# Attention, a mixture of attention experts and a channel mixing in one kernel: other tables for the order of the experts' stage

## The chip, the core and the metric

The kernel runs on one core of a Trainium2 chip. A core has TensorE (PE, matrix products), VectorE (DVE), ScalarE (ACT) and GpSimd (POOL), each with a queue of its own that runs in order, and SyncE (SP), from whose queue the DMAs of this kernel are issued. Results of TensorE land in PSUM and are copied from there to SBUF by VectorE or ScalarE. The metric is the device time of one execution in microseconds (us). It was 1124.65 us for the kernel before, the median of three runs (1122.15 to 1127.39).

## The reference

Three layers follow each other, all on 4 batches and in float32 (the weights of the third layer come as 64-bit floats and are decoded on the chip):

```python
# 1: attention, 8 heads of 64, 1152 rows pooled by 2 to 576 queries
q_pool = q.reshape(B, H, S // 2, 2, D).mean(axis=3)
attn_out = softmax(scale * q_pool @ k.T) @ v                 # (4, 8, 576, 64)
x = attn_out.transpose(0, 2, 1, 3).reshape(4, 576, 512)
# 2: four experts, each a causal attention head of width 64; a row takes two
logits = x @ w_gate                                          # top 2 of 4, softmax of those
for e in range(4):
    q, k, v = x @ wq[e], x @ wk[e], x @ wv[e]
    ye = softmax(causal(scale * q @ k.T)) @ v @ wo[e]
    out += gate_e * ye
# 3: mixing along the rows by rank 32, then along the channels
u = out + (out.T @ U @ V).T
result = u + relu(u @ w_ch1) @ w_ch2                         # 512 -> 2048 -> 512
```

## The kernel before

**The stages.** A first stage computes layer 1 in 16 units (batch times pair of heads) and ends near 480 us. The experts' stage follows, near 480 to 735 us. The channel mixing is the rest; its first units run at the end of the experts' stage. Float32 precision is kept by splitting an operand into a rounded part and a remainder (xh and xl, oh and ol, x2h and x2l, uh and ul, hh and hl) and by adding three products: a copy on ScalarE gives the first part (L226) and a subtraction on VectorE the second (L227).

**A job and its units.** The experts' stage has 8 jobs: 4 batches times 2 expert pairs (ep). Job j has 8 units, one for each half of the queries and each block of 128 keys. A unit's `score` is products st (L871, L872 and the causal mask L876), exp on ScalarE, and sums of the exponentials over the blocks on GpSimd (acc, L885 and L888); its `pv` multiplies with the values (L896). After the last unit of a half, `post_a` sums acc over the partitions (L903), `post_r` and `post_b` turn that into a reciprocal times gate (L432 to L445) and scale the result (L913) into oh and ol.

**What is prepared beside it.** While job j runs, `prep_b(j + 1)` makes the next job's inputs as steps of their own: `cuts` split x by column block (4 steps), `vals` project the values and the gate of a new batch (6 steps), and `projs` (15 steps) are four projections (keys then queries, columns 0 to 320 and 320 to 576), nine score maxima `mxs(t)`, and two `dmax` that write the shifted maxima into q2a and q2b (L399). A maximum is one product (L817) of 64 queries of two heads with up to 512 key columns, and a reduction on VectorE (L820, L824). The maxima get wider with t: 64 to 576 columns; those over 512 are two pieces. The second scores product, L872, reads q2a and q2b, so a job's scores wait for its dmax.

**The mixing.** `mix(b)` has 11 steps: x2(0) to x2(4), tt, hh(0) to hh(4). x2(t) multiplies oh and ol of a batch by wo (6 products of 512 columns), copies the result, splits it into x2h and x2l and adds it to a running product with MUP (L948). tt takes the sum to SBUF as ts (three ACT copies L954, one VectorE subtraction L955). hh(t) multiplies ts back (L961), adds it to x2 (L962), and after the last two the rows are written to u_d in DRAM, from where the channel mixing loads them.

**The tail.** Beside the last job the first weights of the channel mixing are loaded and decoded from 64 bits (`split`, raw to w: six VectorE operations L243 to L248 per half block of 128x512, then a copy on ACT and a subtraction on GpSimd L227), the first rows are turned (L1155) and split, and `mlp(0, fi)` computes the first layer (`up`, L1199, relu L1202, remainder hl L1203) and, one unit later, the second (`down`, L1218).

**What sets the order.** `stream` walks through ticks, three for two units, and issues the units' scores and products and the steps placed at that tick. A step's tick is from a table: CUT_AT, VAL_AT and PRJ_AT[1] for a job that brings a new batch, PRJ_AT[0] for the second pair of a batch, counted from the start of the job beside which the preparation runs; MIX_AT for the mixing of the batch before; MIX_END for the mixing of the last batch, counted from the last job's start like EARLY (opening of the pools and loads of the tail), CW (four weight blocks), CT (turn) and CM (four `mlp` units). The lists are read in the order of the steps given above. A job is 12 ticks long.

```python
for at, g in zip((CUT_AT, VAL_AT, PRJ_AT[1]) if new else ([], [], PRJ_AT[0]), steps):
    place(side, [(3 + t * .75 if j == 0 else t, y) for t, y in zip(at, g)], s0)
if j % EP == 0 and j:
    place(side, list(zip(MIX_AT, mix(j // EP - 1))), s0)
...
place(side, list(zip(MIX_END, mix(B - 1))), sl)
```

This stage isn't under the manual schedule of the others: the framework's scheduler takes the issued order and arranges each engine's row again by its estimates and by when buffers come free. What each engine then has in its row is shown with the change.

**Buffers.** All projections, values, maxima, denominators, output products, hh, turns and first layers write into three PSUM buffers named ms, in turn: a product waits until the third one back has been read. pv has two PSUM buffers, of which the mixing holds one for its running product. x2h and x2l have two buffers each, and so has the raw 64-bit weight.

Of the kernel before, what the change touches and what calls it, by code (L numbers as in the profile page):

```python
# [38 lines left out]
XP_AT = [18, 19, 21, 22, 25, 26, 27, 28, 29, 30, 31, 32, 33, 34, 35]  # L39


CUT_AT = [0, 0, 0, 0]
VAL_AT = [0, 2, 5, 5, 6, 13]
PRJ_AT = [[3, 7, 0, 4, 4, 8, 4, 9, 5, 9, 7, 7, 7, 9, 10], [6, 6, 0, 4, 6, 6, 6, 6, 8, 8, 6, 6, 14, 13, 14]]

MIX_AT = [9, 11, 11, 11, 11, 17, 18, 24, 20, 28, 32]
MIX_END = [14, 17, 18, 21, 23, 25, 39, 32, 31, 41, 38]

EARLY = 5
CW = [7, 20, 23, 37]  # L50
CT = 7
CM = [7, 25, 32, 49]

LATE = 0

# [4 lines left out]
def place(side, steps, t0):  # L60
    for t, g in steps:
        side.setdefault(t0 + int(t), []).append(g)
# [24 lines left out]
def stream(units, side):  # L87

    n = len(units) // 2
    later = {}

    def run(t):
        for g in later.pop(t, []) + side.get(t, []):
            x = g()
            for d, y in enumerate(x if isinstance(x, tuple) else (x,)):
                if callable(y):
                    later.setdefault(t + 1 + d, []).append(y)

    i = 0
    end = max(side, default=0)
    while i <= n or later or 3 * i <= end:
        if i < n:
            units[2 * i][0](0)
            units[2 * i][0](1)
        run(3 * i)
        if i < n:
            units[2 * i + 1][0](0)
        run(3 * i + 1)  # L110
        if i < n:
            units[2 * i + 1][0](1)
        if i % 2 == 0 and 0 < i <= n:
            for x in units[2 * i - 4:2 * i]:
                x[1]()
                if x[2]:
                    for d, y in enumerate(x[2]):
                        later.setdefault(3 * i + 4 + d, []).append(y)
        run(3 * i + 2)
        i += 1  # L120
# [3 lines left out]
def kernel(  # L124
# [795 lines left out]
    def x2_tile(b):  # L920
        if b not in X2:
            X2[b] = xpool.tile([P, NTT - 1, DM], F32, name="x2", tag="x")
        return X2[b]
# [55 lines left out]
    for j in range(NJ):  # L979
        s0 = SA + j * ns  # L980
        units += [unit_b(j, h, kt) for h in range(2) for kt in KT[h]]
        if j + 1 < NJ:
            new = (j + 1) % EP == 0
            steps = prep_b(j + 1, "sv" if new else "s")
# [4 lines that stand above are left out]
    sl = SA + (NJ - 1) * ns  # L989
    place(side, list(zip(MIX_END, mix(B - 1))), sl)  # L990

# [11 lines left out]
    def u_tiles(x, pool_, **kw):  # L1003
        if x == 1:
            u = pool_.tile([P, NC * T], F32, name=f"u{x}", **kw)
            U[x] = u[:, :NS * DM].rearrange("p (s d) -> p s d", s=NS)
            SPARE.append(u[:, NS * DM:NS * DM + 2 * TB].rearrange("p (y t) -> p y t", y=2))
        else:
            U[x] = pool_.tile([P, NS, DM], F32, name=f"u{x}", **kw)
        UH[x] = pool_.tile([P, NC, TB], F32R, name=f"uh{x}", **kw)  # L1010
        UL[x] = pool_.tile([P, NC, TB], F32R, name=f"ul{x}", **kw)
# [65 lines left out]
    def split(fi):  # L1077
        for x, g in enumerate([weights(fi, x) for x in range(2)]):
            gs, end = g()
            for y in gs:  # L1080
                y()
            end()
            keep(fi, x)
# [61 lines left out]
    def load_u(x):  # L1145
        if x > 1:
            U[x] = ct["u"].tile([P, NS, DM], F32, name="u")
        nc.sync.dma_start(U[x], u_d[x * TB:(x + 1) * TB, :].rearrange("(s p) d -> p s d", p=P))
# [9 lines left out]
    def turn(x, c):  # L1158
        turned.add((x, c))
        cut(turn_(x, c), UH[x][:, c, :], UL[x][:, c, :])  # L1160
# [72 lines left out]
    def mlp(x, fi):  # L1233
        hl = up(x, fi)
        if pend:
            down(*pend.pop())
        pend.append((x, fi, hl, [W[fi][:, 1, a, :] for a in range(2)]))
        if x == 0 and fi < 4:
            for y in range(fi + 1):
                if 1 in U and (1, y) not in turned:  # L1240
                    turn(1, y)
# [14 lines left out]
    def seven(p, k, late, more):  # L1256
# [37 lines left out]
        if late:  # L1294
# [21 lines left out]

    place(side, [(EARLY, open_early), (EARLY + 1, lambda: load_u(0)),
                 (EARLY + 4, lambda: (x2_tile(B - 1), u_tiles(1, xpool, tag="x"), load_u(1)) and None)], sl)
    place(side, [(t, lambda fi=fi: split(fi)) for fi, t in enumerate(CW)], sl)
    place(side, [(CT, lambda c=c: turn(0, c)) for c in range(NC)], sl)  # L1320
    place(side, [(t, lambda fi=fi: mlp(0, fi)) for fi, t in enumerate(CM)], sl)
    stream(units, side)
    n = len(CM)
    NK = NF // 2
# [103 lines left out]
```

## Time and profile before

| | |
|---|---|
| median of three runs | 1124.65 us (1122.15 to 1127.39) |
| the profiled execution | 1122.36 us |
| its span | 1120.6 us |
| mean granted clock of TensorE | 0.992 |
| TensorE busy in the span | 1081.5 us |
| VectorE, ACT, POOL busy | 812.8, 542.3, 614.2 us |
| TensorE busy in 480 to 740 us | 246.85 of 260 us |

The profile is of one execution, read after it by several views: the page with the busy time of each engine and the chain of work that ended last; the busy time by stretches; the waits, by the line that waits and the line it waits for; groups of like instructions by line; and the timeline of single instructions. A figure behind "x" is a count of instructions. A matmul's end is modelled, so that two neighbours overlap in the timeline; the distance of two starts tells how long one takes of TensorE.

### The profile page before, as it was taken

The page shows a single profiled execution, that of the slowest core. Times are in us where ns is not written, and L with a number is a line of the kernel's source. Part 1 is how long each engine was busy: PE and PEld are TensorE (multiplying, and loading weights), DVE is VectorE, ACT ScalarE, POOL GpSimd, SP SyncE. Part 2 cuts the span into 40 slices and gives each one's busy share as a digit, 9 for nine tenths or more (in the row PEclk, how much of TensorE's full clock was granted, in tenths as well). Part 3 has the DMA queues.
Part 4 walks back from the last instruction along what each step waited for, and adds up shares of the span by engine and source line. Part 5 has one row for each costly group of instructions (what it writes and reads, how often), then busy time and mean ns, then how long its engine had stood idle before and what let it go on. Part 6 is the DMA issues. An engine that isn't in the chain of part 4 may idle for free.

```text
span 1120.6 us, 19602 instructions
## 1 busy us (share of the span) xinstructions
PE 1081.5 (97%) x6652; PEld 887.4 (79%) x6652; DVE 812.8 (73%) x1707; ACT 542.3 (48%) x1361; POOL 614.2 (55%) x620
## 2 busy tenths in 40 slices
PE   6999999999999999899999999899998999999998
PEld 4777777777777777678787876689887988998987
DVE  6777777888888777656858588979879455565444
ACT  4555666555555555543454535434445445433231
POOL 6888999988888888854424243200009596800000
PEclk8999999999999999999999999999999999999999
DMA  6878897778777765111203044576754755575431
GB/s 144 193 179 185 184 205 175 171 169 193 171 171 166 172 151 117 43 35 38 58 23 106 14 117 148 165 225 195 233 197 169 245 179 188 183 264 202 169 123 57
DMA packets 135157, 171.50 MB, mean 153 GB/s; under 512 B 72464, under 2 KB 88848, under 8 KB 133008
## 3 DMA queue, kind: packets, MB, share of 16 engines
q1 hardware_dynamic: 135056, 170.24, 55.7%
q8 instruction: 53, 0.87, 0.3%
q14 instruction: 48, 0.39, 0.1%
HBM read 83.06 MB, written 32.51 MB: 103 GB/s over the span
## 4 chain that ended last, share of the span: by engine, by line
PE 82%; DVE 8%; POOL 4%; issue 2%; ACT 2%; DMA 2%; SPq 0%; POOLq 0%; ACTq 0%; DVEq 0%
PE o L1218 14%; PE pv L626 12%; PE ms L1268 9%; PE ms L745 9%; PE st L606 8%; PE ms L558 7%; PE st L607 6%; PE ms L1199 5%; PE pv L896 2%; PE ms L633 2%; DVE mp L560 1%; PE ms L506 1%; PE ms L817 1%; DVE xl L227 1%; PE st L872 1%
## 5 line engine op out<-in xcount | busy, mean ns | idle before, releaser
L618 POOL TENSOR_TENSOR acc<-acc,pt 128x576 f32<-128x576 f32 x224 | 319.6, 1427 | 34.3 <-ACT pt L608 18.9
L608 ACT ACTIVATE pt<-st 128x288 f32<-128x288 f32 x576 | 220.0, 409 | 186.1 <-PE st L607 139.3
L560 DVE TENSOR_REDUCE mp<-ms 128x1 f32<-128x384 f32 x432 | 215.1, 549 | 57.6 <-PE ms L558 55.6
L626 PE MATMUL pv<-pt,vr 128*64 128x288 f32 x1152 | 152.3, 409 | 0.0
L558 PE MATMUL ms<-kn,bd 128*128 128x384 f32 x432 | 145.3, 358 | 3.6 <-DVE mp L560 1.7
L626 PEld LDWEIGHTS pv<-pt,vr 128*64 128x64 f32 x1152 | 80.1, 137 | 55.4 <-issue 3.8
L1218 PE MATMUL o<-w,hh 128*128 128x512 f32 x384 | 120.2, 394 | 2.0 <-ACT hh L1202 1.7
L606 PE MATMUL st<-q1a,s1a 128*128 128x288 f32 x288 | 93.7, 325 | 2.8 <-ACT pt L608 2.0
L606 PE MATMUL st<-q1b,s1b 128*128 128x288 f32 x288 | 92.6, 321 | 0.2 <-ACT pt L608 0.2
L558 PEld LDWEIGHTS ms<-kn,bd 128*128 128x128 f32 x432 | 79.9, 191 | 14.8 <-DVE mp L560 6.3
L607 PE MATMUL st<-q2a,s2a 128*128 128x288 f32 x288 | 85.5, 297 | 0.0
L607 PE MATMUL st<-q2b,s2b 128*128 128x288 f32 x288 | 85.1, 296 | 0.0
L1268 PE MATMUL ms<-bc,w 128*128 128x384 f32 x432 | 84.7, 341 | 0.0
L1218 PEld LDWEIGHTS o<-w,hh 128*128 128x128 f32 x384 | 71.5, 188 | 13.9 <-ACT hh L1202 2.0
L1268 PEld LDWEIGHTS ms<-bc,w 128*128 128x128 f32 x432 | 77.6, 190 | 3.0
L1218 PE MATMUL o<-w,hl 128*128 128x512 f32 x192 | 75.5, 393 | 0.9 <-DVE hl L1203 0.9
L606 PEld LDWEIGHTS st<-q1a,s1a 128*128 128x128 f32 x288 | 54.4, 189 | 25.2 <-issue 21.7
L888 POOL TENSOR_TENSOR acc<-acc,pt 128x576 f32<-128x576 f32 (+4 forms) x48 | 45.9, 956 | 49.7 <-ACT pt L879 47.8
L1199 PE MATMUL ms<-uh,w 128*128 128x384 f32 x256 | 71.8, 340 | 1.3 <-ACT sg L1173 1.0
L1218 PE MATMUL o<-w,hs 128*128 128x512 f32 x288 | 71.4, 392 | 0.0
L615 POOL TENSOR_TENSOR acc<-pt 128x576 f32<-128x576 f32 x32 | 50.7, 1586 | 34.8 <-ACT pt L608 34.8
L227 POOL TENSOR_TENSOR bc<-sg,bc 128x384 fp32r<-128x384 f32 x6 | 7.0, 1171 | 106.8 <-ACT bc L226 104.2
(241 smaller groups left out, 2416.9 us busy)
## 6 DMA issues: line engine op xcount, KB each, us to landing
raw<-in_moe_w_ch_dram SPq DMA_DIRECT2D x32, 512.0 KB
w_d<-cb SPq DMA_DIRECT2D x40, 256.0 KB
qr<-in_q_dram SPq DMA_DIRECT2D x16, 576.0 KB
vr<-in_v_dram SPq DMA_DIRECT2D x16, 576.0 KB
s1a<-kn SPq DMA_DIRECT2D x31, 288.0 KB
s1b<-kn SPq DMA_DIRECT2D x31, 288.0 KB
kr<-in_k_dram SPq DMA_DIRECT2D x30, 288.0 KB
wv<-v_d SPq DMA_DIRECT2D x8, 1024.0 KB
```

Of the source, the lines that this page charges most:

```text
L558: nc.tensor.matmul(ps[:, :384], BD[i % 2][:, t, :], KN[i % 2][:, c * 384:c * 384 + 384], start=True, stop=True)
L560: nc.vector.tensor_reduce(st["mp"][:, t, c:c + 1], ps[:, :384], axis=X, op=ALU.max)
L606: nc.tensor.matmul(ps[:, :HT], pr.S1[a][:, ks], pr.Q1[a][:, qs], start=True, stop=False)
L607: nc.tensor.matmul(ps[:, :HT], pr.S2[a][:, ks], pr.Q2[a][:, qs], start=False, stop=True)
L608: nc.scalar.activation(c["pt"][:, a, :], ps[:, :HT], AF.Exp, scale=0.0625)
L615: nc.gpsimd.tensor_add(t, acc[i, h], c["pt"])
L618: nc.gpsimd.tensor_add(acc[i, h], acc[i, h], c["pt"])
L626: nc.tensor.matmul(o[64 * a:64 * a + 64, :HT], vr[:, a, kt, :], c["pt"][:, a, :], start=(kt == 0), stop=(kt == NKT - 1))
L745: nc.tensor.matmul(ps, stat[x][s], mov[x][m], start=(x == 0 and y == 0), stop=(x == n - 1 and y == 2))
L1199: nc.tensor.matmul(ps[:, :TB], W[fi][:, 0, a, cs], m[:, c, :], start=(c == 0 and y == 0), stop=(c == NC - 1 and y == 2))
L1218: nc.tensor.matmul(ob[x][s_], hl[m][:, r], w2[a], start=(n == 0 and y == 0), stop=(n == NF - 1 and y == 2))
L1268: nc.tensor.matmul(ps[:, :TB], w[:, i * HD2 + c * P:i * HD2 + c * P + P], b[:, j, c, :], start=(c == 0 and y == 0), stop=(c == HC - 1 and ...
```

## The change

Only tables are changed. The same instructions are issued, in other places. Step by step: the projections of the second pair of a batch (PRJ_AT[0]) start a tick sooner and its maxima are spread up to tick 15; those of a new batch begin with the two key and query projections of columns 0 to 320 at tick 3, and values come from tick 4; the mixing of a batch (MIX_AT) has its x2 one or more ticks sooner and its tt and hh all by tick 19; the last batch's mixing (MIX_END) is spread to tick 94; the tail's tables (EARLY, CW, CT, CM) have other ticks.

```diff
-CUT_AT = [0, 0, 0, 0]
-VAL_AT = [0, 2, 5, 5, 6, 13]
-PRJ_AT = [[3, 7, 0, 4, 4, 8, 4, 9, 5, 9, 7, 7, 7, 9, 10], [6, 6, 0, 4, 6, 6, 6, 6, 8, 8, 6, 6, 14, 13, 14]]
-
-MIX_AT = [9, 11, 11, 11, 11, 17, 18, 24, 20, 28, 32]
-MIX_END = [14, 17, 18, 21, 23, 25, 39, 32, 31, 41, 38]
-
-EARLY = 5
-CW = [7, 20, 23, 37]
-CT = 7
-CM = [7, 25, 32, 49]
+CUT_AT = [0, 0, 0, 1]
+VAL_AT = [4, 4, 4, 5, 6, 12]
+PRJ_AT = [[2, 7, 0, 2, 2, 5, 5, 7, 6, 11, 8, 13, 9, 12, 15], [3, 8, 3, 7, 5, 7, 6, 7, 5, 9, 10, 11, 14, 10, 15]]
+
+MIX_AT = [8, 8, 8, 10, 11, 11, 18, 17, 15, 18, 19]
+MIX_END = [18, 29, 30, 30, 31, 38, 42, 74, 52, 94, 45]
+
+EARLY = 4
+CW = [5, 9, 21, 27]
+CT = 6
+CM = [9, 17, 36, 50]
```

**First place: TensorE beside job 4, the maxima of job 5.** Before, the maxima pieces of 384, 448 and 512 columns (L817) stand among the PV products (L896):

```order
L896 MATMUL pv<-pt,vl_6828 64x288 x2
L896 MATMUL pv<-pt,vl_6828 64x160
L817 MATMUL ms<-knb,bdb 128x384
L817 MATMUL ms<-knb,bdb 128x448
L896 MATMUL pv<-pt,vl_6828 64x160
L896 MATMUL pv<-pt,vl_6828 64x32 x2
L896 MATMUL pv<-pt,vl_6828 64x288
L817 MATMUL ms<-knb,bdb 128x512
L896 MATMUL pv<-pt,vl_6828 64x288
L871 MATMUL st<-q1a_6469,s1a_6461 128x192
```

Now 384 stands behind the PV products and before the output products of the mixing (wo), of which 18 follow in a row:

```order
L896 MATMUL pv<-pt,vl_6828 64x288 x2
L896 MATMUL pv<-pt,vl_6828 64x160 x2
L896 MATMUL pv<-pt,vl_6828 64x32 x2
L896 MATMUL pv<-pt,vl_6828 64x288 x2
L817 MATMUL ms<-knb,bdb 128x384
L745 MATMUL ms<-wo_108,oh_6846 128x512
L745 MATMUL ms<-wo_109,oh_6846 128x512
L745 MATMUL ms<-wo_108,ol_6848 128x512
L745 MATMUL ms<-wo_108,oh_6847 128x512
```

The pieces of 512 and 448 columns moved behind these output products.

**Second place: VectorE ahead of job 4's first scores.** q2a and q2b with 64x320 are written for those scores (L399). Before they stand behind the maxima of 448 and 320 columns and are the last thing before the old job's denominator (L432):

```order
L820 ISA ms,mx<-ms,mask_m 128x448
L820 ISA mx 128x1
L962 TENSOR_TENSOR x_7766<-ms,x_7766 128x512
L820 ISA ms,mx<-ms,mask_m 128x320
L820 ISA mx 128x1
L399 TENSOR_TENSOR q2a_6471<-negid,mx 64x320
L399 TENSOR_TENSOR q2b_6472<-negid,mx 64x320
L432 STREAM_TRANSPOSE d_8185<-ms 128x288
```

Now they stand ahead of steps of the gate (g_) and of the remainder of the second key projection (klob):

```order
L820 ISA ms,mx<-ms,mask_m 128x256
L820 ISA mx 128x1
L387 TENSOR_TENSOR q1a_6469<-ms,q1a_6469 64x256
L387 TENSOR_TENSOR q1b_6470<-ms,q1b_6470 64x256
L399 TENSOR_TENSOR q2a_6471<-negid,mx 64x320
L399 TENSOR_TENSOR q2b_6472<-negid,mx 64x320
L774 TENSOR_REDUCE g_m<-g_d 128x5
L775 TENSOR_SCALAR g_m<-g_m 128x5
L776 RECIPROCAL g_m<-g_m 128x5
L777 TENSOR_TENSOR g_g<-g_d,g_m 128x20
L368 TENSOR_TENSOR klob<-ms,knb 128x256
L432 STREAM_TRANSPOSE d_8199<-ms 128x288
```

The two L399 moved ahead, and the wider maxima behind them.

**Third place: VectorE where the first weight is decoded (dca, dcb from raw).** Before, the decode begins between the remainders of batch 2's mixing (x2l), ahead of its ts (L955) and its additions (L962):

```order
L227 TENSOR_TENSOR x2l<-ms,x2h 128x512 x2
L243 TENSOR_SCALAR dca<-raw 128x512
L246 TENSOR_SCALAR dcb<-raw 128x512
L244 TENSOR_SCALAR dca<-dca 128x512
L227 TENSOR_TENSOR x2l<-ms,x2h 128x512
L245 TENSOR_SCALAR dca<-dca 128x512
L246 TENSOR_SCALAR dcb<-raw 128x512
L247 SCALAR_TENSOR_TENSOR dcb<-dca,dcb 128x512
L248 SCALAR_TENSOR_TENSOR dcb<-raw,dcb 128x512
L243 TENSOR_SCALAR dca<-raw 128x512
L955 TENSOR_TENSOR ts<-pv,ts 32x512
```

Now it comes behind ts and behind four of the five additions:

```order
L955 TENSOR_TENSOR ts<-pv,ts 32x512
L399 TENSOR_TENSOR q2b_6843<-negid,mx 64x256
L962 TENSOR_TENSOR x_9179<-ms,x_9179 128x512
L432 STREAM_TRANSPOSE d_9384<-ms 128x288
L962 TENSOR_TENSOR x_9179<-ms,x_9179 128x512
L434 TENSOR_SCALAR d_9386<-d_9384 128x9
L962 TENSOR_TENSOR x_9179<-ms,x_9179 128x512
L435 RECIPROCAL d_9386<-d_9386 128x9
L962 TENSOR_TENSOR x_9179<-ms,x_9179 128x512
L437 TENSOR_TENSOR d_9386<-d_9386,g_w 128x9
L243 TENSOR_SCALAR dca<-raw 128x512
L246 TENSOR_SCALAR dcb<-raw 128x512
```

The additions moved ahead of the decode. On TensorE, in rows that are not shown, the first layer of the channel mixing's first unit stands at row 3014 of 3926 instead of 3001 of 3932, that of the second at 3032 instead of 3073, and the output products of the last batch, which stood ahead of the second unit's first layer, follow behind it.

## Rows read from the trace of the kernel before

**Rows 1.** The page: busy time by engine; the chain by engine.
```profile
PE 1081.5 (97%) x6652; PEld 887.4 (79%) x6652; DVE 812.8 (73%) x1707; ACT 542.3 (48%) x1361; POOL 614.2 (55%) x620
PE 82%; DVE 8%; POOL 4%; issue 2%; ACT 2%; DMA 2%; SPq 0%; POOLq 0%; ACTq 0%; DVEq 0%
```

**Rows 2.** Busy time by 20 us: stretch, length, engines (instructions), clock, DMA share, GB/s.
```profile
500.00:520.00 20.00, 17.98 (x122) 14.65 (x123) 14.67 (x35) 8.00 (x20) 7.88 (x11) 0.91 0.17 40
...
540.00:560.00 20.00, 18.53 (x120) 13.94 (x119) 18.01 (x47) 9.14 (x23) 7.14 (x9) 1.00 0.25 59
...
600.00:620.00 20.00, 18.58 (x111) 13.54 (x110) 17.65 (x47) 10.00 (x24) 5.83 (x7) 1.00 0.38 111
...
680.00:700.00 20.00, 17.89 (x123) 12.54 (x123) 19.29 (x38) 11.07 (x26) 10.36 (x10) 1.00 0.26 79
700.00:720.00 20.00, 17.28 (x82) 12.42 (x78) 18.86 (x41) 11.51 (x23) 4.35 (x4) 1.00 0.60 192
720.00:740.00 20.00, 19.44 (x95) 16.27 (x96) 16.93 (x31) 5.84 (x12) 3.46 (x3) 1.00 0.50 158
sum 260.00, PE 246.85 PEld 198.15 DVE 194.89 ACT 120.06 POOL 95.35; mean PE 18.99 PEld 15.24 DVE 14.99 ACT 9.24 POOL 7.33
```

**Rows 3.** Waits of TensorE, 480 to 735 us: total us, times, longest.
```profile
PE ms L817 <- DVE mx L820: 4.2, 4, 1.6
PE ms L1155 <- DVE x L962: 1.7, 1, 1.7
PE o L1218 <- ACT hh L1202: 1.7, 1, 1.7
PE st L872 <- DVE q2b L399: 1.6, 3, 0.5
```

**Rows 4.** Busy time by 4 us, columns as in Rows 2.
```profile
504.00:508.00 4.00, 3.44 (x18) 2.60 (x19) 3.60 (x13) 0.77 (x2) 1.45 (x2) 0.70 0.25 59
```

**Rows 5.** Timeline at the maxima of jobs 1 and 5: start, us, instruction, [idle before].
```profile
504.56 0.51 PE L817 MATMUL ms<-knb,bdb 128*128 128x512 f32 x1 [1.62 <-DVE mx L820]
...
608.12 1.67 DVE L227 TENSOR_TENSOR ol<-o,oh 128x288 fp32r<-128x288 f32 x1
608.43 0.82 PE L896 MATMUL pv<-pt,vl 128*64 128x160 f32 x8
610.37 0.50 PE L817 MATMUL ms<-knb,bdb 128*128 128x512 f32 x1 [1.12 <-DVE mx L820]
```

**Rows 6.** Timeline of the tail, single instructions of VectorE and TensorE.
```profile
680.04 0.42 DVE L243 TENSOR_SCALAR dca<-raw 128x512 int32<-128x512 int32 x1
...
711.72 0.63 PE L745 MATMUL ms<-wo,oh 128*128 128x512 f32 x2
...
731.81 0.55 DVE L1203 SCALAR_TENSOR_TENSOR hl<-ms,hh 128x384 fp32r<-128x384 f32 x1
```

**Rows 7.** Groups on VectorE, 480 to 735 us: count, busy us, mean ns, idle before.
```profile
L962 DVE TENSOR_TENSOR x<-ms,x 128x512 f32<-128x512 f32 x16 | 10.8, 680 | 5.4 <-PE ms L961 5.4
L227 DVE TENSOR_TENSOR ol<-o,oh 128x288 fp32r<-128x288 f32 x16 | 10.2, 639 | 3.2 <-ACT oh L226 3.1
L399 DVE TENSOR_TENSOR q2b<-negid,mx 64x320 fp32r<-64x320 f32 x7 | 5.6, 804 | 0.2
L820 DVE CUSTOM_DVE_ANT_0 ms<-ms,mask_m 128x512 f32<-128x512 f32 x7 | 5.0, 717 | 0.0
L955 DVE TENSOR_TENSOR ts<-pv,ts 32x512 fp32r<-32x512 f32 x4 | 2.7, 680 | 5.7 <-PE ms L745 2.8 <-ACT ts L954 2.8
```

**Rows 8.** Timeline ahead of job 4's second scores product.
```profile
589.75 3.30 POOL L888 TENSOR_TENSOR acc<-acc,pt 128x576 f32<-128x576 f32 x3
591.56 1.18 DVE L399 TENSOR_TENSOR q2b<-negid,mx 64x320 fp32r<-64x320 f32 x1
592.79 0.40 PE L872 MATMUL st<-q2b,s2b 128*128 128x288 f32 x1 [0.52 <-DVE q2b L399]
```

**Rows 9.** The line that copies ts: count, ns min/median/max, first and last start.
```profile
L954 ACT ACTIVATE ts<-pv x12: 585/587/589, 568.2 to 718.3; 32x512 fp32r<-32x512 f32 x12
```

## The prediction

> **What bounds the kernel now.** I read the page first, for which engine carries the span. TensorE is busy 97% of it, and 82% of the chain that ended last is TensorE work; VectorE carries 8% of that chain [rows 1]. A new order of the same steps can therefore only win back time in which TensorE pauses or runs slowly. The second view, busy time by 20 us over the stage that the tables govern (480 to 740 us), says how much that is: TensorE is busy 246.85 of 260 us, so 13.15 us are idle, and they sit in few stretches: 2.0 us in 500 to 520, 1.5 in 540 to 560, 1.4 in 600 to 620, and 2.1 and 2.7 in the two stretches of the tail, 680 to 720; VectorE is busiest in just those stretches (18.0 and 17.7 of 20 us in the middle, 19.3 and 18.9 in the tail) [rows 2]. The tail, 680 to 740, has 5.4 us of the idle time and the part ahead of it 7.8. The third view, the waits of TensorE, names them: 4.2 us before a score-maximum product (L817) until VectorE had read an older one (L820), 1.6 us before a score product (L872) until VectorE had written the shifted maxima (q2b, L399), and 1.7 us before a turn (L1155) and 1.7 before a second-layer product (L1218) in the tail [rows 3]. The fourth view is the granted clock: 0.70 in 504 to 508 us, a stretch that begins with the longest of the L817 waits, 1.62 us, in front of the product at 504.56; at 0.70 in 4 us about 1.2 us of work is lost, and TensorE counts as busy there, so this comes on top of the idle time [rows 4, 5]. The ceiling is then near 14.5 us, of which 9 lie ahead of the tail.
>
> **Part 1: the score maxima of the second expert pair of each batch (PRJ_AT).** All projection, value, maxima, denominator and mixing products take turns in three PSUM buffers named ms. Before, the pieces of 384, 448 and 512 columns come within ten instructions of each other, so the third buffer round meets VectorE's queue. At 607 us: VectorE spends 1.67 us in one subtraction (ol) before it reaches the maxima; the eight PV products of 0.82 us are all that covers it; TensorE stands 1.12 us before the 512 piece [rows 5]. The same form stands in jobs 1, 3 and 5 and makes almost all of the 4.2 us. In the new order, the 384 piece is followed by 18 output products of the mixing, and the 512 piece comes behind those. Two output products of 512 columns take 0.63 us where one takes 0.40, so one follows the other by 0.23, and 18 of them cover 4.1 us [rows 6], against 1.67 plus about 0.72 for the longest maximum [rows 5, 7]. The wait goes in jobs 3 and 5. Job 1 has no mixing beside it, so there the pieces have only values and scores between them: I leave 0.5 us. Where a wait goes, the next buffer user is late instead; with the pieces apart I leave 0.2 us in each of the other jobs. Gain 4.2 - 0.5 - 0.4 = 3.3, bounds 1.5 and 4.2.
>
> **Part 2: the shift by the maxima just before the next job's first scores.** Before, the last small maximum (320 columns) and the two L399 of 64x320 stand directly ahead of the first scores that read them: TensorE stands 0.52 us at 592.79 because q2b took 1.18 us instead of the 0.80 that is its mean [rows 7, 8]. Three such waits make 1.6 us [rows 3]. In the new order both L399 stand in VectorE's row behind the 256-column maximum, and TensorE has eight PV products (0.82 us, rows 5), a projection of 12 products and the last scores of the old job ahead of the first reader. That covers two L399 of 1.2 us at their worst but for a little. Gain 1.5, bounds 0.8 and 1.6.
>
> The Trainium skill (SBUF — State Buffer, on the shared port pair) says that a VectorE instruction with two SBUF inputs and a GpSimd instruction that reads SBUF lock each other out for the whole instruction. The trace agrees at this place: q2b (1.18 us) began while GpSimd's accumulation of 3.30 us ran [rows 8]. By that rule a new order decides nothing by itself: each of these operations can again begin under an accumulation, and parts 1 and 2 would come back elsewhere at some 1 us a hit; this is a mechanism of the first rival below.
>
> **Part 3: the clock.** If the 1.6 us pause before the dip is gone, the dip may go too. The trace has just this one in the stage, so I take 0.8 of its 1.2 us; bounds 0 and 1.2 [rows 4].
>
> **Part 4: the smaller pauses ahead of the tail.** Of the 7.8 us idle ahead of the tail, 5.8 are the two waits above; the other 2.0 are shorter pauses, one or two at a line. The same crowding makes them, and products whose modelled ends run into each other may hide some more; I take 1.5, bounds -0.5 and 2.5.
>
> **Part 5: what the new order adds (MIX_AT).** The last maxima now stand between L948 products, and the first hh (L961) follows soon after the last L948. Ahead of it lie three ACT copies of 0.587 us and one subtraction of 0.68, 2.4 us in a chain, counted without the hops between engines [rows 7, 9]; ahead of it on TensorE stand eight PV products and some short scores, between 1.5 and 2.5 us. Queued behind a waiting L961 is the next job's first projection, and so everything. I price it at 0.5 us for each of three batches: a loss of 1.5, bounds 0 and 4. VAL_AT and CUT_AT move the value products and one cut; their copies out of PSUM are the same in number and lie beside projections: nothing, bounds -0.5 and 0.5.
>
> **Part 6: the tail (MIX_END, EARLY, CW, CT, CM).** VectorE is the limit there: in the 51.8 us from the first decode step (680.04) to the fourth unit's hl (731.81) it is busy nearly all the time [rows 2, 6]. The steps are the same in number. New is that four additions of the mixing of batch 2 (L962, 0.68 us each, 2.7 us) stand ahead of the first decode instead of behind it, and that three of the last batch's five hh come after the fourth unit's first layer. The decode starts later by about that, and less of VectorE's work is left behind it. On TensorE the first unit's first layer stands at row 3014 instead of 3001 and the second's at 3032 instead of 3073, so the second unit is asked for before its weights can be decoded: a new wait of 2 to 4 us there, and the output products of the last batch, now behind it, fill what were waits at L1155 and L1218 (3.4 us together) [rows 3]. On SP the DMAs are the same; the one write of batch 2's mixing that the reload of its rows depends on moves with hh, and stays some microseconds ahead of the turn. I take a gain of 1.5, bounds -4 and 5.
>
> **Sum.** 3.3 + 1.5 + 0.8 + 1.5 - 1.5 + 1.5 = 7.1 us, some half of the ceiling. The profiled execution took 1122.36 us (1.8 more than its span) and would take 1115.3; it lies 2.3 us under the median of the runs shown, and from that median, 1124.65, the forecast is 1117.5.
>
> **The rivals.**
> *The waits only move.* VectorE's work is unchanged, and a hit on ol or q2b costs about 1 us wherever an accumulation happens to run; ol shows it in its mean, 0.64 us over 16, against single ones far above [rows 5, 7]. Then parts 1 and 2 give 2.5 instead of 4.8, the clock and part 4 nothing, part 5 costs 2.5, the tail gives 1: a gain of 1, 1123.6. For it: the collisions belong to timing, not to order. Against it: the new order gives up to 4 us of cover where there was 0.8.
> *The tail gives its waits too.* If the turn of the second unit's input and the output products fill the tail as meant, its gain is its whole idle time of 5.4 us instead of 1.5, part 4 gives 2 and part 5 costs nothing: 7.1 + 3.9 + 0.5 + 1.5 = 13, 1111.6. For it: the new order puts TensorE work that needs no decode behind the second unit. Against it: VectorE is as full as before, and full at 95%.
> *Slower: the decode starts late.* One mechanism: the first decode waits in VectorE's row behind the four L962, these wait for hh, hh for ts, and ts for the L948 products between the scores. Up to its start VectorE stands idle with the raw weights landed. Some of a later start is absorbed: 3.4 us of VectorE's work (four L962 and the L955 before them, 0.68 each) are done ahead, 2.0 us (three L962) are left behind, and about 2.5 us are its idle time in 51.8 at 38.2 busy of 40 [rows 2, 6, 7]. From a start that is 8 us later than now, counted from the last-but-one job's first scores, the rest falls on the end. With a start 13 us later and 5 us of collisions between the decode and the accumulations and weight cuts on GpSimd it costs 10 us, against 5 gained ahead: 1129.7. For it: the order does put these ahead. Against: they were the last thing between the jobs before, too, and their wait is a few microseconds.
> *Not what it says.* That the channel mixing begins sooner holds for its second unit, not for its first by the order on TensorE; if the decode decides, nothing begins sooner. This is in the first and the third rival and has no case of its own.
>
> **How the numbers follow.** Forecast 0.44, waits only move 0.27, tail too 0.17, slower 0.12. About 0.5%, 5.6 us, is what a measurement of this kernel can tell from no change. The forecast's own range is 1114 to 1121, of which some 0.32 is more than 5.6 us under the median; with the tail's 0.17 and 0.05 of the first rival that is 0.54 for faster. Same gets the other 0.12 of the forecast, 0.20 of the first rival and 0.02 of the slower one, 0.34; slower 0.12, with 0.02 of the first rival. The range that leaves out 2 in 10 goes from 1109.5 (half of the tail's case below it) to 1126.5.
>
> **What the profile would show.** Part 1 is right if TensorE's waits at L817 on L820 fall from 4.2 to about 1 us, and wrong if they are above 2.5. Part 2: no wait at L872 on q2b. Part 3: no slice at a clock under 0.9 near the second job. Part 5: a wait at L961 on ts in each batch, about 0.5 us. Part 6: VectorE busy over 90% from first decode to the fourth hl, that stretch 45 to 49 us instead of 51.8, and a wait at the second unit's L1199 on its weights. The prediction is wrong if TensorE idles in the stage as long as before, 13 us, or under 5.

## The result: 1.0% faster, and the profile after

The changed kernel took 1110.70 us, the median of six runs (1109.62 to 1115.79); the kernel before, timed beside it, 1124.63 us (1121.47 to 1127.39). The ratio is 0.9898 with a 95% interval of 0.9883 to 0.9913, so the change is worth 11.5 us (9.8 to 13.2). The forecast was 7.1 us and a time of 1117.5; the time lies under the forecast's own range (1114 to 1121) and inside the wider one (1109.5 to 1126.5). The execution whose profile follows took 1115.27 us (span 1113.5), one of the two slower ones of the six. Its first stage, with the same instructions as before, ended 3.2 us later than in the profile of before: the first job's first product of 160 columns starts at 485.59 instead of 482.43. Differences are therefore counted from that product.

Busy time by 20 us after the change, with the columns of [rows 2]:

```profile
500.00:520.00 20.00, 18.76 (x136) 14.79 (x136) 15.85 (x41) 9.27 (x23) 10.48 (x18) 1.00 0.27 64
...
540.00:560.00 20.00, 19.95 (x129) 16.11 (x129) 16.89 (x45) 11.95 (x28) 7.03 (x10) 1.00 0.23 54
...
600.00:620.00 20.00, 19.95 (x126) 15.39 (x125) 17.31 (x39) 13.77 (x30) 5.91 (x7) 1.00 0.13 30
...
680.00:700.00 20.00, 16.50 (x80) 11.45 (x81) 19.32 (x41) 6.39 (x14) 7.51 (x6) 0.91 0.48 151
700.00:720.00 20.00, 18.19 (x81) 14.03 (x81) 18.63 (x37) 10.38 (x20) 4.20 (x3) 1.00 0.44 136
720.00:740.00 20.00, 18.77 (x85) 16.41 (x84) 12.13 (x23) 5.87 (x12) 1.28 (x1) 0.91 0.60 198
```

Ahead of the tail TensorE has almost stopped pausing (18.53 and 18.58 of 20 us became 19.95 twice), and the clock of 0.91 beside the second job is gone. In the tail it pauses as before, and two stretches have a clock of 0.91 that had 1.00 in [rows 2]. Over 480 to 740 us TensorE idles 8.5 us instead of 13.15.

The waits of TensorE after the change, 475 to 730 us (total us, times, longest):

```profile
PE ms L961 <- DVE ul L227: 1.4, 2, 0.9
PE ms L817 <- DVE mx L820: 1.2, 2, 1.0
PE ms L1199 <- POOL w L227: 1.1, 2, 0.6
PE pv L896 <- DVE o L913: 0.9, 1, 0.9
```

The wait at L817 fell from 4.2 to 1.2 us, that at L872 on q2b (1.6) is gone [rows 3]; the new lines are all in the tail. The 1.2 us that are left all stand beside the first job (at 506.94 and 510.20 us).

Now one stretch that holds the same work in both: from the first job's first product of 160 score columns to the last job's. Busy time by stretches, the kernel before and then the changed one:

```profile
482.43:681.08 198.65, 191.39 (x1317) 156.73 (x1316) 138.63 (x393) 92.39 (x225) 74.88 (x153) 0.99 0.25 68
```

```profile
485.59:669.24 183.65, 182.27 (x1318) 155.13 (x1317) 135.84 (x385) 93.81 (x227) 73.92 (x153) 1.00 0.27 73
```

The stretch is 15.0 us shorter with the same number of TensorE instructions but one. TensorE's idle time fell from 7.3 to 1.4 us; the other 9.1 us came out of its *busy* time. From the last job's product to the end of the span the change costs 4.7 us (1120.6 - 681.08 = 439.5 before, 1113.5 - 669.24 = 444.3 after). So the pair of profiles reads: -3.2 in the first stage, +15.0, -4.7, in sum the 7.1 us between the spans.

How can a busy TensorE win 9 us? The group of the PV products (L896) in the same two stretches, count, busy us and mean ns, before and after:

```profile
L896 PE MATMUL pv<-pt,vl 128*64 128x288 f32 (+4 forms) x208 | 24.6, 347 | 0.0
```

```profile
L896 PE MATMUL pv<-pt,vl 128*64 128x288 f32 (+4 forms) x208 | 20.8, 343 | 0.0
```

The mean of one is nearly the same and the busy time of 208 is 3.8 us less. Busy time counts an overlap once, and a matmul's modelled time reaches over the start of the next one, so a group gets shorter when its products stand in fewer rows. They do: by the starts in the traces, another line follows one of the 208 products 20 times before and 13 times after, while inside a row the next product starts 92 and 85 ns later in the mean. This is order, not pause.

Short pauses that the modelled ends reach over are there too. One such place in the kernel before, ahead of the first scores of job 2 (timeline: start, us, instruction):

```profile
532.85 1.31 DVE L399 TENSOR_TENSOR q2a<-negid,mx 64x320 fp32r<-64x320 f32 x1
533.77 0.38 PE L871 MATMUL st<-q1a,s1a 128*128 128x288 f32 x1
534.21 0.40 PE L872 MATMUL st<-q2a,s2a 128*128 128x288 f32 x1
```

L872 needs q2a and starts 0.44 us after L871. No idle time is printed for it; the same pair starts 0.21 us apart where q2a is ready (591.51 and 591.72 at job 4). Such a place costs 0.2 us and shows in no view of waits. But these pairs make little of the whole: with the printed waits taken out, L872 starts 131 ns after L871 in the mean before and 122 ns after, some 0.9 us in the stretch.

How the busy time divides can be estimated from the starts. Take, for each pair of neighbouring TensorE instructions of given tiles and shapes, the shortest distance of their starts in any trace of this case. These distances add up to 153.3 us over the stretch in the old order and to 147.9 in the new one. So up to 5.4 us may be won because cheaper neighbours stand together, with no pause in it (a pause that comes back at a pair in every trace would still be counted). A part of this is seen directly: a 128*128 product behind a 128*64 one (L896, L903) starts 0.336 us after it, the median in both traces, and the stretch has 26 such places instead of 31. How the busy time divides between cheaper neighbours and hidden pauses is not shown beyond this estimate.

### The profile page after: what moved, and what is told of

Its sections match the earlier page's. It is cut to its first block, busy times and chain, and to the rows that moved or that the text cites. A ratio compares the mean times of both kernels' runs of the same rounds, so it can differ in the third digit from the quotient of the medians.

```text
span 1113.5 us, 19597 instructions
## 1 busy us (share of the span) xinstructions
PE 1078.2 (97%) x6652; PEld 889.9 (80%) x6652; DVE 811.9 (73%) x1707; ACT 542.8 (49%) x1361; POOL 613.1 (55%) x620
## 4 chain that ended last, share of the span: by engine, by line
PE 82%; DVE 7%; POOL 5%; DMA 3%; issue 2%; ACT 2%; SPq 0%; POOLq 0%; ACTq 0%; DVEq 0%
PE o L1218 13%; PE pv L626 12%; PE ms L745 9%; PE ms L1268 8%; PE st L606 8%; PE ms L558 7%; PE st L607 6%; PE ms L1199 5%; PE pv L896 2%; PE ms L633 2%; PE st L871 1%; DVE mp L560 1%; POOL cb L227 1%; PE ms L506 1%; PE st L872 1%
## 5 line engine op out<-in xcount | busy, mean ns | idle before, releaser
L1199 PE MATMUL ms<-uh,w 128*128 128x384 f32 x256 | 74.1, 350 | 2.8 <-POOL w L227 1.1
```

The lines of the kernel that those rows point to most:

```text
L1199: nc.tensor.matmul(ps[:, :TB], W[fi][:, 0, a, cs], m[:, c, :], start=(c == 0 and y == 0), stop=(c == NC - 1 and y == 2))
```

## The experiments

Each kernel below was profiled too. The table has its ratio to the kernel before on the same chip with the interval, the stretch of jobs (as above, between the first and the last job's first product of 160 columns, read from the timeline) and the rest of the span behind it. Where the mixing has other ticks than in the change, some of its work lies on the other side of that border, and only the sum compares.

| kernel | ratio (95%) | jobs, us | rest, us |
|---|---|---|---|
| before | 1 | 198.6 | 439.5 |
| the change | 0.9898 (0.9883 to 0.9913) | 183.6 | 444.3 |
| prep_only | 1.0010 (0.9998 to 1.0022) | 193.9 | 448.0 |
| mix_only | 1.0102 (1.0073 to 1.0131) | 197.7 | 450.4 |
| tail_only | 1.0013 (0.9999 to 1.0028) | 198.8 | 442.4 |
| prep_and_mix | 0.9902 (0.9877 to 0.9926) | 183.6 | 443.1 |
| old_second | 1.0085 (1.0054 to 1.0116) | 197.7 | 449.0 |
| old_batch | 0.9956 (0.9942 to 0.9970) | 191.0 | 442.1 |
| old_mixend | 0.9905 (0.9882 to 0.9929) | 183.6 | 444.7 |
| old_start | 0.9904 (0.9879 to 0.9929) | 183.6 | 443.9 |
| after_act | 0.9900 (0.9876 to 0.9923) | 183.7 | 444.6 |
| before_no_acc | 0.9901 (0.9878 to 0.9923) | 190.8 | 437.1 |
| after_no_acc | 0.9845 (0.9826 to 0.9864) | 180.8 | 441.9 |
| late_hh | 0.9947 (0.9926 to 0.9968) | 183.7 | 449.7 |

**One group of tables alone.** Theory A: the gain is made ahead of the tail. Rival B: the tail's tables make it. Rival C: the tables only work together.

```diff
 # prep_only: before with
+CUT_AT, VAL_AT, PRJ_AT of the change
 # mix_only: before with
+MIX_AT of the change
 # tail_only: before with
+MIX_END, EARLY, CW, CT, CM of the change
 # prep_and_mix: before with
+CUT_AT, VAL_AT, PRJ_AT, MIX_AT of the change
```

> Only CUT_AT, VAL_AT and PRJ_AT are changed. Theory A (the gain is made ahead of the tail, mostly by the spread of the preparation): 6 to 10 us faster than before. Rival B (the tail's tables make the gain): within 2 us of before. Rival C (the tables only work together): slower than before by 2 us or more, since the mixing then meets the spread maxima at its old ticks.

> Only MIX_AT is changed. Theory A: 0 to 4 us faster, the pauses at the maxima stay. Rival B: within 2 us. Rival C: slower by 2 us or more.

> Only MIX_END, EARLY, CW, CT and CM are changed. Theory A: 0 to 5 us slower, since in the traces the stretch from the last job's narrow scores to the end is 4.6 us longer after the change. Rival B: 5 to 12 us faster. Rival C: about as before, for the last job has no preparation beside it.

> CUT_AT, VAL_AT, PRJ_AT and MIX_AT are changed, the tail keeps the tables of before. Theory A: 11 to 16 us faster than before, as fast as the whole change or up to 4 us faster. Rival B: within 3 us of before. Rival C: 5 to 8 us faster, half of the whole change.

Rival B falls: the tail's tables alone give nothing (1.0013), and without them the other four give the whole change (0.9902 against 0.9898). Theory A is right on the place, wrong on the shares: the preparation alone gives nothing (it said 6 to 10 us) and the mixing alone costs 11.5 us (it said 0 to 4 won), while both together win 11. So Rival C's idea holds for these two, though its number does for mix_only alone: prep_only is 1.1 us slower, not 2 or more. (Of the mixing's x2 steps the last one keeps its tick, 11, in both tables; the other four are sooner.) The profile of prep_only shows where the preparation's gain goes. Up to job 6 it is ahead (159.6 us from the first job's product to that of job 6, against 170.6 before), and there the old ticks of the mixing put an addition behind the two L399, and the first output products behind that. The timeline of that place:

```profile
657.02 1.63 DVE L399 TENSOR_TENSOR q2a<-negid,mx 64x320 fp32r<-64x320 f32 x1
658.67 1.29 DVE L399 TENSOR_TENSOR q2b<-negid,mx 64x320 fp32r<-64x320 f32 x1
660.62 0.73 PE L745 MATMUL ms<-wo,oh 128*128 128x512 f32 x2 [2.48 <-DVE x2e L962]
```

Busy time by 4 us behind it, columns as in [rows 2]:

```profile
664.00:668.00 4.00, 4.00 (x12) 3.23 (x13) 2.44 (x7) 1.38 (x4) 0.45 (x1) 0.50 1.05 394
```

TensorE waits 2.48 us, up to 660.62. The granted clock is 0.73 in 660 to 664 us, and then a whole 4 us stretch runs at half the clock: 1.2 instead of 2.4 GHz.

**One half of the preparation at its old ticks.**

```diff
 # old_second: the change with
-PRJ_AT[0] = [2, 7, 0, 2, 2, 5, 5, 7, 6, 11, 8, 13, 9, 12, 15]
+PRJ_AT[0] = [3, 7, 0, 4, 4, 8, 4, 9, 5, 9, 7, 7, 7, 9, 10]
 # old_batch: the change with
+CUT_AT, VAL_AT, PRJ_AT[1] of before
```

> The changed kernel with the preparation of the second expert pair (PRJ_AT[0]) at its old ticks. Theory A (each half of the preparation gives its own share ahead of the tail): the pauses beside jobs 0, 2, 4 and 6 come back, 4 to 8 us slower than the whole change, 4 to 8 us under before. Rival C (the spread maxima and the sooner mixing only work together): 10 us or more slower than the whole change, as fast as before or slower, since the mixing's products then stand among the crowded maxima.

> The changed kernel with the preparation of a new batch (CUT_AT, VAL_AT, PRJ_AT[1]) at its old ticks. Theory A: the pauses beside jobs 1, 3 and 5 come back (4.2, 1.5 and 1.5 us by the traces), 4 to 8 us slower than the whole change. Rival C: 10 us or more slower than the whole change.

old_batch came out as Theory A said: the stretch of jobs is 7.4 us longer than in the change, of which 5.3 stand beside job 1 (24.7 us there in the change, 30.0 here). old_second is Rival C: it loses the whole gain and 9.6 us more. So the pair that needs each other is the preparation of the second expert pair and the mixing, which run beside the same jobs. Waits of TensorE in the stretch of jobs of old_second:

```profile
PE ms L817 <- DVE mx L820: 4.8, 6, 1.6
PE pv L948 <- DVE o L913: 1.2, 2, 0.6
PE ms L817 <- DVE klob L368: 0.8, 2, 0.4
```

A reading that fits: crowded maxima and sooner mixing products now share the three ms buffers in the same microseconds, while the old mixing came behind the maxima and the new maxima leave room for the new mixing. It is shown only in part: TensorE idles 9.0 us in this stretch instead of 1.4 in the change, and the stretch is 14.1 us longer.

**The additions of GpSimd left out.** Theory L: VectorE's collisions with them make the pauses of before. Rival O: the crowding makes them, at VectorE's free speed too.

```diff
-                nc.gpsimd.tensor_add(t, t, c["pt"][:nk, :, c0:])
+                pass
```

> The kernel before without the additions of GpSimd in the experts' stage (L888: the sums of exponentials hold only their first block, so the output is another). Theory L (the pauses before come from VectorE's operations that run into these additions, and the change covers them): 6 to 12 us faster than before. Rival O (the crowding of the maxima in the row makes them, at VectorE's free speed too): within 3 us of before.

> The changed kernel without the same additions. Theory L: little is left to win, 0 to 3 us faster than the changed kernel, 11 to 15 us under before, so that order is worth 2 to 5 us once the additions are gone. Rival O: as far below its counterpart as the change is below before, 9 to 13 us.

The stretch of jobs in before_no_acc and in after_no_acc, columns as above:

```profile
481.80:672.60 190.80, 188.87 (x1318) 156.12 (x1316) 129.32 (x393) 92.06 (x225) 35.78 (x111) 1.00 0.26 71
```

```profile
482.30:663.10 180.80, 180.76 (x1318) 154.76 (x1318) 127.81 (x385) 93.46 (x227) 34.38 (x111) 1.00 0.28 74
```

The additions cost 7.9 us of it before (198.65 - 190.80) and 2.9 after (183.65 - 180.80). So of the 15.0 us that the order wins there, 10.0 are won without any addition, and 5.0 hang on them. (Taking the additions out also frees GpSimd and ends their reads; the experiment doesn't part that from the collisions.) Over the whole kernel the order is worth 6.3 us without the additions (0.9901 to 0.9845) and 11.5 with them. before_no_acc came out as Theory L said. after_no_acc fits neither: it is 6.0 us under the change, where Theory L allowed 3, and 6.3 under before_no_acc, where Rival O wanted 9 to 13.

The pauses themselves are Theory L's. TensorE's largest wait in the old order without the additions, 480 to 672 us:

```profile
PE ms L817 <- DVE mx L820: 0.7, 2, 0.4
```

It was 4.2 us with them, and no wait at L872 on q2b is left (1.6 with them) [rows 3]. So the crowding at VectorE's free speed makes 0.7 of the 4.2 us. The 10.0 us are mostly not pauses: TensorE's idle time in the two stretches is 1.9 us (190.80 - 188.87) and 0.0, and 8.1 us (188.87 - 180.76) came out of its busy time, at a clock of 1.00 in both. Neither theory named that. By the estimate above most of it can come from the order of the products on TensorE itself; no kernel here tests that alone.

Whether the change avoids collisions or covers them is seen on VectorE. Without the additions its busy time in the stretch falls by 9.3 us in the old order (138.63 to 129.32) and by 8.0 in the new one (135.84 to 127.81), so most of the collisions are still there. They hit other instructions. Groups after the change, 480 to 735 us, with the columns of [rows 7]:

```profile
L399 DVE TENSOR_TENSOR q2a<-negid,mx 64x320 fp32r<-64x320 f32 x7 | 9.2, 1311 | 0.2
L227 DVE TENSOR_TENSOR ol<-o,oh 128x288 fp32r<-128x288 f32 x16 | 8.0, 497 | 3.2 <-ACT oh L226 3.1
```

The same q2a group without the additions (before_no_acc, 475 to 735 us):

```profile
L399 DVE TENSOR_TENSOR q2a<-negid,mx 64x320 fp32r<-64x320 f32 x7 | 3.4, 490 | 0.2
```

q2a takes 490 ns free, 759 in the kernel before and 1311 in the change: it collides more than before, and no TensorE wait names it. ol collides less (497 ns instead of 639 [rows 7]), and so does q2b (483 instead of 804). The timeline ahead of job 4's first scores in the change:

```profile
583.54 1.41 POOL L888 TENSOR_TENSOR acc<-acc,pt 128x576 f32<-128x576 f32 x1
584.20 1.09 DVE L399 TENSOR_TENSOR q2a<-negid,mx 64x320 fp32r<-64x320 f32 x1
588.00 0.29 PE L872 MATMUL st<-q2a,s2a 128*128 128x288 f32 x1
```

q2a is written 2.7 us before L872 reads it. For q2a this is cover, not avoidance; for ol and q2b the new order also avoids.

**The tail.** In the change it gives back 4.7 us, in prep_and_mix 3.6. Four kernels ask why.

```diff
 # old_mixend: the change with
+MIX_END of before
 # old_start: the change with
+EARLY, CW, CT, CM of before
 # after_act: the change, first decode step of the first four weight blocks on ScalarE
-                if fi >= NW:
-                    gs[0] = lambda: nc.scalar.activation(f(a), f(y[:, :, 1]), AF.Abs) and None
+                gs[0] = lambda: nc.scalar.activation(f(a), f(y[:, :, 1]), AF.Abs) and None
 # late_hh: the change
-            place(side, list(zip(MIX_AT, mix(j // EP - 1))), s0)
+            place(side, list(zip(MIX_AT[:6] + [24, 22, 28, 30, 32] if j == NJ - 2 else MIX_AT, mix(j // EP - 1))), s0)
```

> The changed kernel with the last batch's mixing (MIX_END) at its old ticks. Theory F (the tail gives back 3 to 5 us whichever tables it has): within 2 us of the whole change. Rival G (the end of the mixing between the units is what keeps the tail short): 3 to 6 us slower than the whole change.

> The changed kernel with the loads, weights, turns and first units of the channel mixing (EARLY, CW, CT, CM) at their old ticks. Theory F: within 2 us of the whole change. Rival G: 3 to 6 us slower, since the last batch's mixing, spread for units that begin sooner, then comes late.

> The changed kernel, with the first step of each 64-bit decode of the first four weight blocks (an absolute value, 0.41 us, eight of them in the tail) on ScalarE instead of VectorE. Theory D (VectorE's work sets the end of the tail: from the last-but-one job's narrow scores to the fourth unit's hl it is 78.7 us in both traces, whatever the tables): 3.3 us less for VectorE, the tail 2 to 3.5 us shorter, 13 to 15 us under before. Rival E (the tail's length is from TensorE's own order and its clock): within 1 us of the changed kernel, 10.5 to 12.5 us under before.

> The changed kernel with the five hh of batch 2's mixing 6, 5, 13, 12 and 13 ticks later (24, 22, 28, 30, 32), those of the other batches as in the change; in VectorE's row the first two weight decodes then stand ahead of all L962. Theory H (the tail gives back 3 to 5 us because the first decode stands behind four additions and starts 7.8 us later than before, counted from the last-but-one job's narrow scores): the decode starts 2.5 to 4 us sooner and the kernel is 2 to 4 us faster than the whole change, 13.5 to 15.5 us under before. Rival F (the tail is VectorE's and TensorE's waits for each other in any order): within 1.5 us of the whole change.

old_mixend and old_start are as fast as the change: Theory F, the tail's tables don't matter beyond what the intervals tell. after_act has VectorE's last decode step of the four blocks done 3.7 us sooner, counted from job 6's first product (75.5 instead of 79.2), and is no faster: Theory D falls. The time is the one Rival E named, whose reason this kernel doesn't show. Its longest wait, and the busy time behind that:

```profile
PE ms L961 <- DVE ts L955: 3.3, 1, 3.3
```

```profile
716.00:720.00 4.00, 4.00 (x15) 3.90 (x13) 1.04 (x2) 0.27 (x1) 1.28 (x1) 0.50 0.32 98
```

TensorE now stands 3.3 us before an hh that waits for ts (and 2.4 us at another place), and then 4 us run at half the clock. late_hh went against its theory and its rival: it is 5.5 us slower than the change (0.9947 against 0.9898), and the first decode hardly came sooner. VectorE ahead of it, and TensorE's longest wait:

```profile
669.06 0.48 DVE L432 STREAM_TRANSPOSE d<-ms 128x288 f32<-128x288 f32 x1 [0.36 <-PE ms L903]
...
671.18 0.48 DVE L445 STREAM_TRANSPOSE d<-d 128x288 f32<-128x288 f32 x1 [0.51 <-ACT d L439]
671.58 0.53 DVE L227 TENSOR_TENSOR ul<-ms,uh 128x384 fp32r<-128x384 f32 x1
672.03 0.42 DVE L243 TENSOR_SCALAR dca<-raw 128x512 int32<-128x512 int32 x1
```

```profile
PE ms L1199 <- DVE x L962: 2.9, 1, 2.9
```

With the four L962 gone, the decode starts 34.2 us after job 6's first product of 160 columns instead of 34.8: the row holds the next denominator's steps ahead of it, which wait for TensorE and ScalarE. The additions then fell among the first units, where TensorE waits for one of them (2.9 us at L1199). That the additions ahead of the decode are the price is not supported; that they aren't could not be settled by this kernel, which hardly moved the decode.

## Why the prediction was right on the sign and short on the size

- **Parts 1 and 2** came out in their sums: 4.2 to 1.2 us at L817 (3.0 won, 3.3 said), 1.6 to 0 at L872 (1.5 said). What is left at L817 stands beside the first job alone, where 0.5 was said, and the other jobs have none.
- **Part 3** (the clock): the dip of 500 to 520 us is gone, 0.09 of 20 us, 1.8 won, 0.8 said and at most 1.2. The sum had taken one slice of 4 us; in the kernel before the next one, 508 to 512, has a clock of 0.87 too.
- **Parts 4 and 5** together were put at nothing (1.5 won, 1.5 lost). What is left of the stretch for them is 15.0 - 3.0 - 1.6 - 1.8 = 8.6 us. Part 5 shows no cost: the only wait at L961 on ts, 0.5 us, lies in the tail. Part 4's shorter pauses were 2.0 us of idle time, of which 1.3 went (5.9 - 3.0 - 1.6). The other 7.3 us (9.1 less the clock's 1.8) came out of TensorE's busy time, and no part had a price for that. The error lies one step earlier, in the sentence that a new order can only win back time in which TensorE pauses or runs slowly: from it came the ceiling of 9 us ahead of the tail, and 15.0 were won. The same reading put the idle stretches down to a busy VectorE; in 500 to 520 us it was busy only 14.67 of 20 us [rows 2].
- **Part 6** had the wrong sign: 1.5 won was said, 4.7 were lost in the profiled pair. What it said of VectorE held in the main: it is busy 95% of the time from the first decode to the fourth hl (41.9 of 43.95 us). The first decode starts 34.8 us after job 6's first product of 160 columns instead of 27.0, and the fourth hl stands 78.7 us after it in both. The timeline of the tail after the change, VectorE and TensorE, and the busy time by 4 us:

```profile
676.80 0.41 DVE L243 TENSOR_SCALAR dca<-raw 128x512 int32<-128x512 int32 x1
...
720.75 0.54 DVE L1203 SCALAR_TENSOR_TENSOR hl<-ms,hh 128x384 fp32r<-128x384 f32 x1
...
721.35 0.49 PE L961 MATMUL ms<-ts,mv 128*128 128x512 f32 x1 [0.56 <-DVE hl L1203]
722.41 0.50 PE L961 MATMUL ms<-ts,mv 128*128 128x512 f32 x1 [0.57 <-DVE ul L227]
```

```profile
684.00:688.00 4.00, 2.63 (x9) 2.31 (x10) 4.00 (x9) 1.10 (x2) 1.44 (x3) 0.80 0.55 185
...
724.00:728.00 4.00, 4.00 (x14) 3.67 (x14) 1.08 (x3) 1.06 (x2) 0.00 (x0) 0.58 0.69 262
```

From decode to hl it is 44.0 us instead of 51.8 (45 to 49 said), so the late start is absorbed, as the third rival's sum allowed up to 8 us. Of the loss of 4.7 us, 0.8 lies ahead of the fourth hl and 4.0 between it and the fifth unit's, which follows 2.3 us later before and 6.3 after:

```profile
734.12 0.56 DVE L1203 SCALAR_TENSOR_TENSOR hl<-ms,hh 128x384 fp32r<-128x384 f32 x1 [1.29 <-ACT hh L1202]
```

```profile
727.06 0.56 DVE L1203 SCALAR_TENSOR_TENSOR hl<-ms,hh 128x384 fp32r<-128x384 f32 x1 [2.91 <-ACT hh L1202]
```

Three hh of the last batch stand at that place on TensorE. Two of them wait for ms buffers, 0.56 and 0.57 us, and then 4 us run at a clock of 0.58 (1.7 us lost). The other dip, 684 to 692 us, lies ahead of the fourth hl.

The new MIX_END has its share in absorbing the late start, since with the old one these three hh stand 4 to 8 us ahead of the fourth hl. In prep_and_mix, with the old MIX_END, the decode starts 35.8 us after job 6's product and the fourth hl stands 81.5 us after it instead of 78.7, while the stretch from there to the end is 388.8 us as before. In tail_only, with the new one, the decode starts at 27.0 and the fourth hl stands at 78.7, but from there to the end it is 391.7 us. So the tail is paid ahead of the fourth hl with the old table and behind it with the new one.

The forecast's wait at L1199 on the weights came, 1.1 us in all where 2 to 4 were said.

- **The rivals.** "The waits only move" is right for the tail alone. "The tail gives its waits too" named 1111.6, near the measured 1110.7, by the wrong mechanism: the tail gave nothing. The late decode happened. The rule of the Trainium skill (SBUF — State Buffer, on the shared port pair) predicted collisions in the new order too, and they are there (1311 ns at q2a). That the order decides nothing by itself did not hold: it decides whether TensorE sees them, and ol and q2b meet fewer.
- **What was luck.** The terms missed in both directions: ahead of the tail 5.6 us were said and 15.0 won, in the tail 1.5 were said to be won and 4.7 were lost. The spans of the two profiles differ by just the 7.1 us of the forecast, but 3.2 us of first stage, which no part of the change touches, are in that.

What stays open is why the tail costs more once the jobs are shorter. Every kernel with the short jobs and the additions has 443.1 to 449.7 us behind the last job's product against 439.5 before; no table of the tail changes it by more than the runs tell, less VectorE work doesn't, and each profile has other waits and mostly one or two stretches of lower clock. Without the additions of GpSimd it is 441.9 against 437.1 with no lower clock in any 20 us of 660 to 740 in either, so the clock alone isn't the cause. No kernel here was clearly faster than the change with the whole output computed.

## What to carry to other kernels

A TensorE that is busy 97% can have more time to win in its busy time than it shows as idle: in short pauses behind an instruction, and in which products stand next to each other. Compare the same stretch of work between two fixed instructions, or the distance of starts with that of an undisturbed pair, before setting a ceiling from idle time. In a row that runs in order, distance between a producer and its reader can pay even when the producer gets slower, as q2a did. And tables that place two sets of steps into the same buffers are one change: here one half alone gave nothing, the other alone cost 11.5 us, and both together won 11.

## What the runs showed of the hardware

A pause of TensorE can cost twice: soon behind one of 2.48 us (prep_only) and one of 3.3 us (after_act) a 4 us stretch ran at 0.50 of the clock, 1.2 GHz. The length of the pause alone doesn't tell: in the kernel before two pauses of 1.7 us in the tail left the clock at 1.00 in every 20 us [rows 2, 3], while behind one of 1.62 us it was 0.70 in 4 us [rows 4, 5]. VectorE's q2a, 490 ns without GpSimd's additions, took 1311 ns on average beside them. A 128*128 product behind a 128*64 one started 0.336 us after it (median), while inside a row of the 128*64 PV products the next one started 92 or 85 ns later in the mean.
